# Opening order of a fused attention and two-MLP kernel: w_out converted one block later, low parts on VectorE, x parts and weight sums made beside the last plain slices, loads held during bursts

## The chip, the core and the metric

The kernel runs on one core of one Trainium2 chip. The metric is the device time of one execution in microseconds, lower is better; it is given as the median of several runs. The engines are named TensorE (matmul; the profile's PE), VectorE (DVE), ScalarE (ACT), GpSimd (POOL) and SyncE (SP, which only issues transfers). TensorE's clock is granted by the chip at one of two levels, 1.2 or 2.4 GHz.

## What is computed

Chunked attention over q, k, v (8 batches, 8 heads, 576 positions, 64 features, chunks of 64), then two gated products one after the other on 4608 tokens of 512 features:

```python
x   = attention(q, k, v)                      # (4608, 512)
x2  = ((x @ w_a) * (x @ w_b)) @ w_out         # 512 -> 1536 -> 512
h   = ((x2 @ w1) * (x2 @ w2)) @ w3            # 512 -> 1024 -> 1024
out = h @ w_out2                              # 1024 -> 512
```

All is float32. The kernel fuses w3 and w_out2 into one matrix first.

## The kernel before, in words

**Numbers.** A float32 product is made of three products of rounded halves: every operand is split into a high part (a ScalarE copy that rounds) and a low part (source minus high part, on VectorE or GpSimd). `split` does both. The raw weights reach the core in another number format and are converted (`Conv`: `s1` is two VectorE operations and a ScalarE one, `s2` a third VectorE operation, L209 to L220). `Pump` runs these conversions as a list of jobs in order: `load` asks for the raw tile, `begin` does `s1`, `run` finishes the job before, does `s2` and hands the result to the job's sink. A w_a or w_b tile is split and its float32 form stored to `d32`; a w_out tile (`out_job`, L745) is split and stored to `dwo`.

**Tokens.** 4608 tokens are 9 blocks of 512. Blocks 0 and 1 are done plainly, one feature block f of 128 at a time (`plain_step`): two banks, `pa` and `pb`, get x @ w_a and x @ w_b, ScalarE copies `pa` to `sa`, VectorE multiplies `pb` by it. For T=0 (block 0) the product is split (`g_parts`) and goes through w_out at once as a `Second`, four parts of three matmuls one step later ("pending"). For T=1 (block 1) it is kept in a `G` tile. The 24 slices run in the order of `plain_order`: five of T=0 first (`AHEAD`), then mixed; the last four are (0, 11), (1, 9), (1, 10), (1, 11). The other blocks go in pairs through Strassen's scheme, seven products where eight would be needed (`strassen_step`), whose x parts come from `strassen_pieces`: 8 differences ("formed") and 14 splits ("one") per pair of blocks, 22 pieces. The sums of weights that the scheme needs are made by `Sums` in the first such block (four adds, two splits and two stores for each f) and reloaded from `dw` later (`load_part`).

**Bursts.** Block j + 1 of a pair has its G tiles multiplied by w_out in one go, `burst` (12 Second products for the first matrix, 8 for the second), before the next pair starts. During a burst VectorE makes the x parts of the next pair, GpSimd the low parts of the G tiles (`ready`), and SP loads `wo` tiles (`Outs.ahead`): four buffers, the last four w_out tiles are still there at the first burst, so its fifth product is the first that needs a load.

**Attention.** A `Unit` is one pair of heads of one token block: load1 (q and k), load2 (v), turn (transposes), scores, soft1, soft2, flip, apply, put. Units 0 to 3 are block 0, units 4 to 7 block 1 (class `First`); the units of the next pair run beside the slices and steps, from fourth product on also in a burst. Loads of q, k and v are put into a list (`ask`), and `tick` issues a few of them with each product; `settle` issues all up to the one needed. While `state["hold"]` is set, `tick` issues none; `burst` sets it at its start and clears it after its first product. `next_units` appends the requests of the next pair's first two units; for the second pair these are 52, put in at slice (1, 9) and issued nine per product (`pace`).

**Order.** Nothing is scheduled by a compiler: each engine runs its instructions in the order in which the program emits them. `Track` spreads pieces of other work over the points of a step: each piece has a cost, and at each `point()` pieces are emitted until their share is done. SP, VectorE and the others each are one queue, in which a waiting instruction holds up all behind it. A tile's buffer is its `tag`: a new tile with the same tag waits for the last reader of the old one.

Of the kernel before, what the change touches and what calls it, by code (L numbers as in the profile page):

```python
# [17 lines left out]
P = 128  # L18
# [92 lines left out]
def chunk_attention_two_gated_products(  # L111
# [434 lines left out]
    class First(TurnedOnPE):  # L546
# [3 lines left out]
        def queues(self):  # L550
            early = self.T == 0 and self.hp < 2
            return nc.sync, *[nc.scalar if early else nc.sync] * 2
# [52 lines left out]
    def strassen_pieces(x32, nm, single=False, diffs=None):  # L605
# [8 lines left out]
        def minus(a, b, name):  # L614
            t = diffs.popleft() if diffs else tmp(name, W)
            nc.vector.tensor_tensor(t, a, b, op=ALU.subtract)
            return t
# [23 lines left out]
        def one(p, kt):  # L641
# [5 lines left out]
        order = [  # L647
            (formed, "P5"),
            (formed, "P6"),
            (one, "P5"),  # L650
            (one, "P1"),
            (one, "P2"),
            (formed, "P7"),
            (one, "P6"),
            (formed, "P4"),
            (one, "P3"),
            (one, "P7"),
            (one, "P4"),
        ]
        return parts, [  # L660
            (0.7, False, lambda do=do, p=p, kt=kt: do(p, kt)) for do, p in order for kt in range(2)
        ]

# [81 lines left out]
    def out_job(f):  # L745
        def sink(w):
            t = pool.tile([P, 2, DM], F32R, tag=f"wo{f % 4}", name=f"wo_{f}")
            wouts[f] = t

            def low():  # L750
                nc.gpsimd.tensor_tensor(t[:, 1], w, t[:, 0], op=ALU.subtract)
                store(dwo[0][f], t.bitcast(F32), 2, nc.gpsimd)

            return (lambda: nc.scalar.copy(t[:, 0], w)), low

        return (row_conv(w_o, f, f"o{f}"), sink)
# [52 lines left out]
    class Sums:  # L809
# [66 lines left out]

        def early_pieces(self):
            return [
                (1.7, False, self.add),
                (0.7, False, lambda: self.own(0)),  # L880
                (0.4, False, lambda: self.own(1)),
                (0.7, False, lambda: self.early(0)),
                (0.7, False, lambda: self.early(1)),
            ]
# [40 lines left out]
    class Second:  # L925
# [6 lines left out]
        def part(self):  # L932
            m, ph, f, w, g = self.m, self.ph, self.f, self.w, self.g
            if m == 4:
                return
# [105 lines left out]
    def plain_step(ph, j, T, f, nm, point, gplaces, sums, tags, xq=None, freed=None):  # L1041
# [5 lines left out]
        pa = bank(tags[0], f"pa{nm}")  # L1047
        first(w, 0, xq, f"pa{nm}", pa)
# [5 lines left out]
        pb = bank(tags[1], f"pb{nm}")  # L1054
        first(w, 1, xq, f"pb{nm}", pb)
# [8 lines left out]
        else:  # L1064
            nc.vector.tensor_tensor(sa, pb, sa, op=ALU.mult)
            engines.computed(0.7)
            g = g_parts(sa, nm, nc.gpsimd)
# [5 lines left out]
            wo = state["outs"].next() if "outs" in state else wouts[f]  # L1073
# [10 lines left out]
    def burst(ph, j, order, gplaces, others, at, first=None):  # L1084
# [10 lines left out]
        for f in range(n):  # L1095
# [10 lines left out]
            if f == 0:  # L1106
                state["pending"].rest()
                parts.append(ready(ph, j, order[2], gplaces))
                state["hold"] = False
# [91 lines left out]
    with tc.manual_schedule():  # L1201
# [4 lines left out]
        for f in range(NF[0]):  # L1206
            pump.add(pair_jobs(f) + [out_job(f)])
# [58 lines left out]
        asked(U[0].load1, U[1].load1)  # L1266
        pump.load()
        asked(U[2].load1, U[3].load1, U[2].load2)
# [16 lines left out]
        AHEAD = 5  # L1285
# [6 lines left out]
        asked(U[0].load2)  # L1292
# [5 lines left out]
        asked(U[1].load2)  # L1298
        U[1].scores()
        U[2].turn()  # L1300
        U[0].soft2()
        U[0].flip()
        U[1].soft1()
        pump.load()
        asked(U[4].load1)
        U[1].soft2()
# [3 lines left out]
        U[3].turn()  # L1310
        U[1].flip()
        U[2].soft1()
        pump.run()
# [22 lines left out]
        def features(m, kks):  # L1336
            terms = [(wp, xp, kk) for kk in kks for wp, xp in SEQ[::-1]]
            some(pairs[0, 0], m, xq, banks[m], terms, kks[0] == 0, kks[-1] == KM - 1)

# [8 lines left out]
        pump.ahead = 2  # L1348
# [8 lines left out]
        pump.ahead = 1  # L1357
        pump.run()
        U[4].soft1()
        pump.flush()  # L1360
        nc.vector.tensor_tensor(sa, banks[1], sa, op=ALU.mult)  # L1361
        state["pending"] = Second(0, 0, 0, wouts[0], g_parts(sa, "0_0_0", nc.gpsimd), sums[0])
        pump.ahead = 2
# [8 lines left out]
        at = None  # L1372
        for n, (T, f) in list(enumerate(order))[1:]:
            if T == 0:
                ahead = f + 1 < AHEAD
                conv = Track([conv_piece()] * (4 if f == 1 else 3), 2 if ahead else 8, engines)
                if f + 1 == NF[0]:
                    conv = None
            if T == 1 and f == 0:
                late.finish()  # L1380
                at = Track(both[cut:], sum(3 if T_ else 5 for T_, _ in order[n:-3]) - 2, engines, 3.0)

            def point(pe=True):
                if conv:
                    conv.point(pe)
                (at or late).point(pe)

            if T == 1:
                for i in [f + 1] if f else [0, 1]:
                    for m in range(2 if i < NF[0] else 0):  # L1390
                        store(dw[0][i][m], whole(pairs[0, i][m]).bitcast(F32), 2, nc.gpsimd)
            if n + 3 == len(order):
                at.finish()
                next_units(2)
                state["pace"] = 9
            if n + 1 == len(order):
                state["ready"] = ready(0, 1, NF[0] - 2, plain[0])
            plain_step(0, 0, T, f, f"0_{T}_{f}", point, plain[0], sums[0], "AC")
# [3 lines left out]
        at.finish()  # L1402

# [15 lines left out]
        def block_steps(ph, sb, x, at):  # L1419
# [10 lines left out]
            for k, f in enumerate(order):  # L1430
                extra = None
                if new:
                    if k + 2 < n:
                        su[k + 2] = summed(ph, order[k + 2], k + 2)
                        su[k + 2].load()
                    extra = Track(su[k + 1].pieces() if k + 1 < n else [], 5, engines, 2.0)
# [7 lines left out]
                def freed(i):  # L1444
                    if k + 2 < n:
                        if whole_new and f + 2 >= READY:
                            return
                        if not new or i in (0, 3):
# [10 lines left out]
                if k + 1 == n and ph == 0 and sb + 1 < NSB:  # L1459
                    for a in at:  # L1460
                        a.finish()
                    next_units(sb + 2)
# [67 lines left out]
        for ph, sb in [(0, sb) for sb in range(1, NSB + 1)] + [(1, sb) for sb in range(NSB + 1)]:  # L1530
# [13 lines left out]
            elif not begins:  # L1544
                x, pieces = strassen_pieces(x32, f"{ph}{sb}", sb == NSB)
            if ph == 0 and sb == 1:
                for n_ in range(2):
                    first_sums[n_] = summed(ph, orders[ph, sb][n_], n_)
                    first_sums[n_].load()
                    for i in (0, 3):  # L1550
                        load_part(ph, orders[ph, sb][n_], i)
                pieces = pieces + first_sums[0].pieces()
# [54 lines left out]
            j, places = block_steps(ph, sb, x, at)  # L1607
# [51 lines left out]
```

## Time and profile before

| | us |
|---|---|
| median of 3 runs | 1606.45 (1604.29 to 1608.12) |
| profiled execution | 1609.44 |
| its span, first to last instruction | 1607.6 |
| mean granted TensorE clock in it | 0.985 of 2.4 GHz |

The profile is of one execution. A line of the timeline gives an instruction, or several alike merged (x8), with start and duration, and in brackets how long its engine was idle before it and what ended that. `SPq`, `ACTq` and the like are an engine's queue issuing a transfer. TensorE's busy time is the sum of its matmuls, which are pipelined, so a busy TensorE at half clock counts as busy too.

### The profile page before, as it was taken

To read this page: it belongs to the slowest core of one execution; us is meant where nothing else is said; L and a number is where in the kernel's file an instruction comes from. 1 tells how busy PE (TensorE), PEld (TensorE's weight loads), DVE (VectorE), ACT (ScalarE), POOL (GpSimd) and SP (SyncE) were. 2 spreads that over 40 slices of the span, in tenths; PEclk is the share of its full clock that TensorE was granted. 3 is DMA by queue.
4 is the path that set the end of the run, shared out by engine and by line. 5 is a ranking of instruction groups with operands and counts; after the bars stand their busy time and mean duration, and the time that the engine had idled before them with its cause. 6 is when DMAs were issued, how large, how long until landed. Compare 5 with 4: busy or idle time off the path is not lost.

```text
span 1607.6 us, 24155 instructions
## 1 busy us (share of the span) xinstructions
PE 1545.6 (96%) x8968; PEld 1255.6 (78%) x8968; DVE 859.0 (53%) x1384; ACT 538.4 (33%) x997; POOL 492.6 (31%) x502
## 2 busy tenths in 40 slices
PE   5799999899899999999999999999999999999998
PEld 4578787677677788887877888888878878878887
DVE  4877564677757555476776345634632432432431
ACT  3544344322233222342334323333421321421322
POOL 0323224222234111343224312224522422422422
PEclk8899999899999999999999999999999999999999
DMA  8798756677646787569985899777366266166184
GB/s 229 230 263 267 245 154 226 211 226 222 208 151 188 203 222 231 142 200 337 323 315 184 296 335 356 288 262 261 112 230 216 76 227 219 68 222 205 68 294 152
DMA packets 277014, 356.31 MB, mean 222 GB/s; under 512 B 174241, under 2 KB 194721, under 8 KB 276897
## 3 DMA queue, kind: packets, MB, share of 16 engines
q1 hardware_dynamic: 244448, 261.43, 52.7%
q0 software_dynamic: 23616, 81.80, 13.3%
q10 hardware_dynamic: 8832, 11.54, 2.1%
q8 instruction: 71, 1.16, 0.3%
q14 instruction: 47, 0.38, 0.1%
HBM read 268.70 MB, written 85.98 MB: 221 GB/s over the span
## 4 chain that ended last, share of the span: by engine, by line
PE 81%; DVE 7%; DMA 4%; issue 3%; ACT 2%; SPq 1%; POOL 1%; DVEq 0%; ACTq 0%; POOLq 0%
PE P L914 39%; PE acc L944 23%; PE pa L901 4%; PE pb L901 4%; PE wf L1189 3%; PE pb0L L901 2%; PE pa0L L901 2%; DVE xP L288 2%; DMA wo<-dwo 2%; PE x L442 1%; SPq L181 1%; PE s L390 1%; DMA qk<-in_k_dram 1%; DMA v<-in_v_dram 1%; ACT xP L287 1%
## 5 line engine op out<-in xcount | busy, mean ns | idle before, releaser
L914 PE MATMUL P<-xP,w 128*128 128x512 f32 (+1 forms) x3066 | 695.3, 380 | 13.5 <-DVE c L1034 5.2
L914 PEld LDWEIGHTS P<-xP,w 128*128 128x128 f32 x3066 | 550.7, 188 | 130.3 <-DVE c L1034 7.5
L1005 DVE TENSOR_TENSOR c<-P,c 128x512 f32<-128x512 f32 (+1 forms) x228 | 150.0, 661 | 320.4 <-PE P L914 319.7
L1001 ACT COPY c<-P 128x512 f32<-128x512 f32 (+1 forms) x228 | 128.2, 563 | 212.7 <-PE P L914 211.5
L1036 POOL TENSOR_TENSOR G<-c,c 128x512 f32<-128x512 f32 x68 | 90.7, 1334 | 312.3 <-DVE c L1005 312.2
L287 ACT CAST gh<-c 128x512 fp32r<-128x512 f32 x68 | 42.2, 621 | 325.2 <-DVE c L1034 325.1
L288 POOL TENSOR_TENSOR gl<-c,gh 128x512 fp32r<-128x512 f32 x68 | 90.7, 1333 | 191.5 <-ACT gh L287 186.0
L944 PE MATMUL acc<-gh,wo 128*128 128x512 f32 x384 | 138.2, 400 | 0.0
L1034 DVE TENSOR_TENSOR c<-P,c 128x512 f32<-128x512 f32 x68 | 47.0, 691 | 124.7 <-PE P L914 124.6
L944 PE MATMUL acc<-wo,gh 128*128 128x512 f32 x320 | 111.0, 390 | 0.5 <-ACT gh L287 0.5
L944 PEld LDWEIGHTS acc<-gh,wo 128*128 128x128 f32 x384 | 72.6, 189 | 15.7
L901 PE MATMUL pa<-xq,w 128*128 128x512 f32 x276 | 72.4, 414 | 6.3 <-DVE w L725 6.3
L288 DVE TENSOR_TENSOR xP<-xP,xP 128x512 fp32r<-128x512 f32 (+1 forms) x56 | 65.7, 1217 | 21.2 <-ACT xP L287 21.2
L944 PE MATMUL acc<-gl,wo 128*128 128x512 f32 x192 | 75.4, 393 | 0.0
L944 PEld LDWEIGHTS acc<-wo,gh 128*128 128x128 f32 x320 | 60.1, 188 | 12.9 <-ACT gh L287 1.0
L901 PE MATMUL pb<-xq,w 128*128 128x512 f32 x276 | 68.8, 398 | 0.8 <-DVE sa L1361 0.8
L901 PEld LDWEIGHTS pa<-xq,w 128*128 128x128 f32 x276 | 53.1, 197 | 19.0 <-DVE w L725 6.9
L954 ACT COPY ev<-acc 128x512 f32<-128x512 f32 x72 | 42.3, 587 | 72.5 <-PE acc L944 67.6
L944 PE MATMUL acc<-wo,gl 128*128 128x512 f32 x160 | 62.5, 390 | 0.8 <-POOL gl L288 0.8
L901 PEld LDWEIGHTS pb<-xq,w 128*128 128x128 f32 x276 | 50.9, 190 | 11.9 <-DVE sa L1361 1.3
L190 POOL DMA_DIRECT2D dw<-w x58 | 31.8, 551 | 91.0 <-DVE w L288 83.0
L408 ACT ACTIVATE e<-e 128x512 f32<-128x512 f32 x36 | 22.8, 634 | 102.2 <-DVE e L402 98.4
(163 smaller groups left out, 2368.0 us busy)
## 6 DMA issues: line engine op xcount, KB each, us to landing
w<-dw SPq DMA_DIRECT2D x175, 512.0 KB, 4.6
wo<-dwo SPq DMA_DIRECT2D x128, 512.0 KB, 4.3
dw<-w POOLq DMA_DIRECT2D x58, 512.0 KB, 4.8
w<-dw SPq DMA_DIRECT2D x59, 256.0 KB, 3.6
su<-d SPq DMA_DIRECT2D x20, 512.0 KB, 5.4
x2d<-ev POOLq DMA_DIRECT2D x36, 256.0 KB, 4.3
x<-x2d SPq DMA_DIRECT2D x36, 256.0 KB, 4.4
out_dram<-ev POOLq DMA_DIRECT2D x36, 256.0 KB, 2.9
```

Source lines behind the costliest of these rows:

```text
L190: queue.dma_start(to, src)
L287: nc.scalar.copy(dst_h, src)
L288: eng_l.tensor_tensor(dst_l, src, dst_h, op=ALU.subtract)
L901: nc.tensor.matmul(ps, w[m][:, kk // 2, wp, kk % 2], xq[kk // 2][:, kk % 2, xp], start=(begins and n == 0), stop=(ends and n == len(terms) ...
L914: nc.tensor.matmul(ps, w[:, wp, kt], x[:, kt, xp], start=(begins and n == 0), stop=(n == 5), skip_group_check=True,)
L944: nc.tensor.matmul(acc[m], a, b, start=(f == 0 and (wp, gp) == SEQ[0]), stop=(f == NF[ph] - 1 and (wp, gp) == SEQ[-1]),)
L954: nc.scalar.copy(t, acc[m])
L1001: nc.scalar.copy(t, src)
L1005: nc.vector.tensor_tensor(o, a, b, op=ALU.add)
L1034: nc.vector.tensor_tensor(g, last, c11, op=ALU.mult)
L1036: nc.gpsimd.tensor_tensor(g_place(ph, nm.split("_")[0], f, gplaces), c22, c12, op=ALU.mult)
L1189: nc.tensor.matmul(ps, t[:, gp, jj], wo2[jj // 2][:, jj % 2, wp], start=(jj == 0 and (wp, gp) == SEQ[0]), stop=(jj == NF[1] - 1 and (wp, g ...
```

## The change

- `First.queues`: unit 0's values are loaded on GpSimd's queue and unit 1's on SP's instead of both on ScalarE's, and both are asked for near the start.
- The jobs of the pump: w_out tile f is converted after w_a and w_b of f + 1. `Second` takes its w_out tile when it starts (`lambda: wouts[f]`).
- Low parts of w_out 0 to 3 and of the hidden tiles of the first slices (f below 5) are made by VectorE instead of GpSimd. The first conversions are begun one ahead instead of two; slices 4 and 10 get four conversions, the others three.
- The first products of slice (1, 0) are issued three matmuls at a time between the last pieces of attention of block 1.
- For EARLY = 3 feature blocks (11, 10, 9) the weight sums are made beside the last four slices into `xo4` to `xo6` and stored to `dw`; the first pair of Strassen blocks reloads them (`load_part` for i = 0 to 3). Two of the three sums' loads share buffer Y0.
- 18 of the 22 x pieces of the first pair are made beside the last three slices, with differences in `Y2`. Before every later pair but the last of each matrix, 8 of 22 pieces are made in the last step ahead of the burst.
- `hold` is cleared after product n - 4 of a burst instead of the first (n = 12 or 8).

```diff
         def queues(self):
-            early = self.T == 0 and self.hp < 2
-            return nc.sync, *[nc.scalar if early else nc.sync] * 2
+            first = self.T == 0
+            return (
+                nc.sync,
+                nc.scalar if first and self.hp < 2 else nc.sync,
+                nc.gpsimd if first and self.hp == 0 else nc.sync,
+            )
...
+    def diff_tiles(name):
+        t = pool.tile([P, 4, NT], F32, tag="Y2", name=name)
+        return deque([*(t[:, i] for i in range(4)), *[None] * 4])
...
             def low():
-                nc.gpsimd.tensor_tensor(t[:, 1], w, t[:, 0], op=ALU.subtract)
+                e = nc.vector if f + 1 < AHEAD else nc.gpsimd
+                e.tensor_tensor(t[:, 1], w, t[:, 0], op=ALU.subtract)
...
+        def staged_pieces(self, tag):
+            def stage():
+                t = pool.tile([P, 2, 4 * NT // 2], F32R, tag=tag, name=f"st{self.f}")
+                self.stage = [
+                    t[:, i].rearrange("p (o s k n) -> p o s k n", o=2, s=2, k=2) for i in range(2)
+                ]
+            return [
+                (1.7, None, lambda: (stage(), self.add())),
+                (0.7, None, lambda: self.parted(0, self.stage[0])),
+                (0.7, None, lambda: self.parted(1, self.stage[1])),
+            ]
...
+        if begun:
+            pa, pb = begun.banks
+            tick(loads=2)
+            begun(0, [KM - 1])
+        else:
+            pa = bank(tags[0], f"pa{nm}")
+            first(w, 0, xq, f"pa{nm}", pa)
...
-            g = g_parts(sa, nm, nc.gpsimd)
+            g = g_parts(sa, nm, nc.vector if early else nc.gpsimd)
...
                 parts.append(ready(ph, j, order[2], gplaces))
+            if f == n - 4:
                 state["hold"] = False
...
-            pump.add(pair_jobs(f) + [out_job(f)])
+            pump.add(pair_jobs(f) + ([out_job(f - 1)] if f else []))
+        pump.add([out_job(NF[0] - 1)])
...
-        asked(U[0].load1, U[1].load1)
+        asked(U[0].load1, U[0].load2, U[1].load1)
         pump.load()
-        asked(U[2].load1, U[3].load1, U[2].load2)
+        asked(U[2].load1, U[1].load2, U[3].load1, U[2].load2)
...
-                conv = Track([conv_piece()] * (4 if f == 1 else 3), 2 if ahead else 8, engines)
+                pump.ahead = 1 if ahead else 2
+                conv = Track([conv_piece()] * (4 if f + 1 in (AHEAD, NF[0] - 1) else 3), 2 if f < AHEAD else 8, engines)
...
             if T == 1 and f == 0:
-                late.finish()
+                xq = [quadrants[1, 0], quadrants[1, 1]]
+                banks = [bank("AC"[m], f"p{m}1") for m in range(2)]
+                chunks = deque((m, [kk]) for kk in range(KM - 1) for m in range(2))
+                while late.left:
+                    piece = late.left.popleft()
+                    piece[2]()
+                    if piece[1] and chunks:
+                        features(*chunks.popleft())
...
+            if n + 4 == len(order):
+                staged = []
+                for i in range(EARLY):
+                    su = Sums(0, NF[0] - 1 - i, dict(tag=f"Y{i % 2}"))
+                    staged.append((0.1, None, su.load))
+                    staged.append(su.staged_pieces(f"xo{4 + i}"))
+                loads = [staged[2 * i] for i in range(EARLY)]
+                pieces = loads[:2]
+                for i in range(EARLY):
+                    pieces += staged[2 * i + 1] + loads[i + 2 : i + 3]
+                st = Track(pieces, 8, engines)
             if n + 3 == len(order):
                 at.finish()
                 next_units(2)
                 state["pace"] = 9
+                got_x, got_pieces = strassen_pieces(
+                    [u.x32 for u in units], "01", diffs=diff_tiles("xd01"),
+                    steps="f5 f6 o1 o2 o3 f7 o7 f4 o4 o5 o6",
+                )
+                state["parts"] = got_x, got_pieces[18:]
+                xt = Track(got_pieces[:18], 8, engines)
...
-                if k + 1 == n and ph == 0 and sb + 1 < NSB:
+                if k + 1 == n and sb + 1 < NSB:
                     for a in at:
                         a.finish()
-                    next_units(sb + 2)
+                    if ph == 0:
+                        next_units(sb + 2)
+                    steps = "f5 f6 o5 o1 o2 f7 o6 f4 o3 o7 o4"
+                    nx, np = strassen_pieces(
+                        next_x32(), f"{ph}{sb + 1}", diffs=diff_tiles(f"xd{ph}{sb}"), steps=steps
+                    )
+                    state["parts"] = nx, np[8:]
+                    extra = Track(np[:8], 6, engines)
...
             if ph == 0 and sb == 1:
                 for n_ in range(2):
-                    first_sums[n_] = summed(ph, orders[ph, sb][n_], n_)
-                    first_sums[n_].load()
-                    for i in (0, 3):
+                    for i in range(4):
                         load_part(ph, orders[ph, sb][n_], i)
-                pieces = pieces + first_sums[0].pieces()
```

## Rows read from the trace of the kernel before

**Rows 1.** The page's first part: busy us of each engine, share, instructions.
```profile
PE 1545.6 (96%) x8968; PEld 1255.6 (78%) x8968; DVE 859.0 (53%) x1384; ACT 538.4 (33%) x997; POOL 492.6 (31%) x502
```
**Rows 2.** Stretches: length, busy PE PEld DVE ACT POOL; last clock, DMA share, GB/s.
```profile
0.00:120.00 120.00, 89.61 (x850) 70.81 (x851) 83.80 (x160) 54.72 (x108) 26.98 (x37) 0.87 0.84 241
40.00:100.00 60.00, 50.23 (x361) 39.09 (x358) 52.40 (x88) 32.51 (x64) 21.29 (x23) 0.91 0.80 242
280.00:300.00 20.00, 14.13 (x81) 10.73 (x81) 17.49 (x32) 4.57 (x8) 6.44 (x6) 0.79 0.57 170
380.00:420.00 40.00, 35.09 (x235) 26.90 (x233) 27.80 (x52) 8.57 (x17) 9.55 (x10) 1.00 0.72 217
500.00:520.00 20.00, 16.87 (x92) 12.95 (x91) 11.21 (x19) 3.93 (x7) 5.21 (x6) 0.83 0.55 147
```
**Rows 3.** Waits of PE, 0 to 120 us: us in total, times, longest.
```profile
PE pa L901 <- DVE w L725: 6.3, 2, 3.9
...
PE x L442 <- DMA v<-in_v_dram: 3.1, 2, 1.7
```
**Rows 4.** Timeline of ScalarE, 10 to 17 us: start, duration, instruction.
```profile
15.86 0.97 ACTq L181 DMA_DIRECT2D v<-in_v_dram  x2
```
**Rows 5.** Timeline of VectorE, 22 to 29 us.
```profile
28.14 0.76 DVE L400 TENSOR_REDUCE mx<-s 128x4 f32<-128x256 f32 x2 [4.66 <-PE s L390]
```
**Rows 6.** Timeline of GpSimd and of VectorE, 70 to 76 us.
```profile
72.19 1.45 POOL L288 TENSOR_TENSOR gl<-sa,gh 128x512 fp32r<-128x512 f32 x1 [4.36 <-ACT gh L287]
...
71.81 0.70 DVE L212 SCALAR_TENSOR_TENSOR cv_xo<-cv_xo 128x512 int32<-128x512 int32 x1
72.42 1.77 DVE L220 SCALAR_TENSOR_TENSOR cv_Y<-cv_Y,cv_Y 128x512 int32<-128x512 int32 x1
```
**Rows 7.** Timeline of TensorE, 102 to 115 us.
```profile
106.52 0.63 PE L530 MATMUL f<-ident,e 128*128 128x128 f32 x4 [1.86 <-DVE e L416]
...
108.88 5.54 PE L901 MATMUL pa<-xq,w 128*128 128x512 f32 x12
```
**Rows 8.** The chain that ended last: start, us, what.
```profile
205.18 2.72 PE acc L944 x12
...
258.95 5.76 PE acc L944 x24
```
**Rows 9.** Timeline of VectorE, 239 to 260 us.
```profile
247.33 0.69 DVE L1061 TENSOR_TENSOR G0p<-pb,sa 128x512 f32<-128x512 f32 x1 [7.97 <-PE pb L901]
```
**Rows 10.** Groups of VectorE, 258 to 292 us: busy us, mean ns, idle before.
```profile
L288 DVE TENSOR_TENSOR xP<-xP,xP 128x512 fp32r<-128x512 f32 x8 | 9.2, 1197 | 4.5 <-ACT xP L287 4.5
```
**Rows 11.** Timeline of VectorE, 286 to 291 us.
```profile
286.30 0.41 DVE L827 TENSOR_TENSOR su<-su 128x256 f32<-128x256 f32 x1
...
289.28 0.70 DVE L378 STREAM_TRANSPOSE qT<-qk 128x512 f32<-128x512 f32 x1
```
**Rows 12.** Timeline of SP, 221 to 263 and 286 to 300 us.
```profile
220.96 4.05 SPq L181 DMA_DIRECT2D qk<-in_q_dram  x8
...
249.59 6.45 SPq L181 DMA_DIRECT2D v<-in_v_dram  x10
...
262.04 0.32 SPq L782 DMA_DIRECT2D wo<-dwo  x1
...
290.60 0.86 SPq L181 DMA_DIRECT2D qk<-in_q_dram  x2
```
**Rows 13.** Transfers, 255 to 300 us: rate in 40 slices; sums' loads, us to landing.
```profile
GB/s 43 65 266 357 339 219 379 404 408 408 412 415 138 7 58 342 66 211 255 117 346 33 335 102 138 328 0 0 0 0 0 259 339 303 297 296 254 291 118 42
...
su<-d SPq DMA_DIRECT2D x2, 512.0 KB, 5.0
```
**Rows 14.** Timeline of VectorE, 460 to 520 us.
```profile
504.09 0.70 DVE L378 STREAM_TRANSPOSE qT<-qk 128x512 f32<-128x512 f32 x1
```
**Rows 15.** Timeline of SP, 477 to 506 us.
```profile
478.57 4.12 SPq L181 DMA_DIRECT2D qk<-in_q_dram  x7
```
**Rows 16.** Waits of PE, 1150 to 1200 us.
```profile
PE P L914 <- DVE c L1005: 0.8, 1, 0.8
```

## What is predicted, and why

> **What bounds the kernel now.** I read the page's busy line first [rows 1]: TensorE works 1545.6 us of a 1607.6 us span. The change takes no matrix product away, so all that it can win is the 62 us in which TensorE stands still and the time in which its clock is granted at 1.2 instead of 2.4 GHz. The second view is the busy time by stretch [rows 2]: the reader sees where those 62 us lie. The opening (0 to 120) has 30.4 of them, 280 to 300 another 5.9, 380 to 420 some 4.9, 500 to 520 3.1. In all of these but 380 to 420 the mean granted clock is below 1.00 too, as TensorE has just stood idle. Third, the waits name what ends the idle time in the opening: the values `v` and converted weights [rows 3].
>
> The loss around a burst is idle time plus the share of the clock that was not granted. At the end of the first burst that is 5.87 + 0.21 x 20 = 10.1 us, at the end of the second 3.13 + 0.17 x 20 = 6.5 us [rows 2].
>
> **The change part by part, 1: the opening.** Three edits meet here.
>
> (a) The values of units 0 and 1. ScalarE's queue issues them behind its own copies now, those of unit 1 at 15.86 us, which holds the next copy back by 0.97 us [rows 4]. TensorE waits 3.1 us for `v` [rows 3], and VectorE stands idle 4.66 us, until 28.14, since the scores behind that wait come late [rows 5]. Afterwards unit 0's values are issued at the start on GpSimd's queue, unit 1's on SP's ahead of unit 3's q and k: behind about 2.3 MB at 241 GB/s [rows 2], so there by some 13 us (an estimate). I take 4 off, ends 0 and 4.7. The Trainium skill, "DMA: Bandwidth & Descriptors", section "Issuing engines are not separate DMA queues", speaks against a gain from another queue: all issuers share the same 16 DMA engines, so only issue time is saved. By it alone this edit would bring ScalarE's issue time, 2 x 0.97 = 1.9 us; I stay at 4 because the order of the loads changes too.
>
> (b) The low parts of `w_out` 0 to 3 and of five hidden tiles go from GpSimd to VectorE, 9 instructions. VectorE pays 0.70 us each, as for its other operations of that size [rows 6]: 6.3. But a GpSimd subtraction lengthens what VectorE does beside it: the L220 that starts 0.23 us after one takes 1.77 us [rows 6], 1.07 more than its neighbour. I found such a stretched operation beside nearly all of the ten subtractions up to 108 us. So 9 x (0.70 - 1.0) = -2.7; ends +6.3 if the relief fails, -3.3 if each gives 1.07. I take -2.
>
> (c) `w_out` 0 is converted behind `w_a` and `w_b` 1. TensorE waits 6.3 us for a converted `w` [rows 3]. But VectorE is busy 52.4 of 60 us here [rows 2], so a new order mostly moves the queue: by the first slice of T=1 both kernels have converted 17 tiles. I take -1, ends 0 and -4.
>
> Sum of part 1: -7, from +3 to -12.
>
> **2: the first slice of T=1.** Unit 7's chain of transposes, softmax and values is emitted whole before it now; TensorE stands 1.86 us in front of one link and then does twelve matmuls in 5.54 us [rows 7], twice the 2.72 us of others [rows 8]. After, six groups of three matmuls stand between the links. If the clock then stays at 2.4 GHz, the slice ends 5.54 - 2.72 = 2.8 earlier for the clock and up to 1.9 for the wait. But slice 4 has four conversions pressed into its first two points, which can hold unit 7 up: -3.5, from 0 to -4.7.
>
> **3: the last slices and the first burst, the term that decides.** Into the slices go, for each of three feature blocks, a load of 512 KB, four adds, two splits and two stores, and 18 of 22 x pieces; these leave the burst. VectorE has gaps of 7.97 us before the first of those slices' multiplications [rows 9] and of some 2 x 2.72 - 0.69 = 4.75 between them. Work there should cost 0.7 per piece, not the 1.2 that it takes in the burst beside GpSimd [rows 10]. The load is 3 x (4 x 0.41 + 2 x 0.7) + 18 x 0.7 = 21.7 us [rows 6, 11] in four slices that hold about 22. It fits, tightly: the multiplication that frees TensorE's second bank queues behind the pieces, so I put 2 us of TensorE waits on the slices. Without those pieces unit 0's transposes, now at 289.28 [rows 11], come early; SP's q load and with it the `wo` load behind it waits for them until 290.60 [rows 12], and hold keeps such loads off SP anyway. So the 10.1 us at the burst's end go; if that were all, the burst would win 8.
>
> But SP is in order, and the sums' loads stand ahead of 52 requests for q, k and v. SP issues those 52 from 220.96 to 256.04 now, then weights, and at 262.04 the `wo` of the burst's fifth product [rows 12], which is needed at 258.95 + 5 x 2.72 = 272.6 (four products and the pending one before it) [rows 8]. After, SP meets first the load of block 11's sums, which waits until that block's float32 store has landed: about 232 (an estimate: that conversion ends at some 227, and a load of this size lands in 5.0 us [rows 13]). Then comes the load of block 9, whose buffer is block 11's: free only after that block's second split, which is emitted behind the first product part of slice (0, 11), at about 238, and follows the 5.0 us load, four adds and a split: about 241.5. Only then come the 52 requests, 20 us later than now. At the 0.51 us of the first eight they need 27 us, at today's mean 35 [rows 12]: done at 268 to 277. Behind them stand eight weight loads of 3.67 MB, 9.0 us at the 408 GB/s of that stretch [rows 13], then the `wo`: landed at 278 to 290. With the slices 2 us late, TensorE stands from 274.6 for 4 to 15 us. I take 9, and 4 for the low clock behind it, as the 5.87 us of idle time cost today. The term: -10.1 + 2 + 9 + 4 = +5, ends -9 (no such wait) and +11.
>
> **4: the second burst.** Eight of 22 x pieces move into the step ahead; 8 x 1.2 = 9.6 us less lie ahead of unit 0's transposes at 504.09 [rows 14], and no q load that waits for them stands ahead of a `wo` load. Of 6.5 lost I take 5, ends -6.5 and 0 (the 16 q and k loads of unit 1 now come ahead of the last `wo`).
>
> **5: the three bursts of the second product.** Each is followed by one wait of 0.8 us for VectorE [rows 16]. Less work there, eight pieces more in the step ahead: -1.5, ends -2.4 and +1.5.
>
> **6: held requests in the third burst and in blocks** (0, 1) to (0, 3). SP gets 25 requests out in the step before a burst; the others start eight products later. The 4.9 us at 380 to 420 [rows 2] lie in the middle of a block, where nothing changes, and stay. 0, from -3 to +4.
>
> Sum: -7 - 3.5 + 5 - 5 - 1.5 + 0 = -12. The profiled execution took 1609.44 us for its 1607.6 span, 3.0 above the median of the three runs; the difference goes onto the median: 1606.45 - 12 = **1594**.
>
> **The rivals.** First, SP's backlog is gone before the fifth `wo`: part 3 gives -9, and the whole 1606.45 - 7 - 3.5 - 9 - 5 - 1.5 = 1580. For it: eight requests take only 4.05 us when nothing disturbs them [rows 12], and weights could land faster. Against: block 9's buffer, which the code ties to block 11's. Second, VectorE's sum of work binds the opening and the relief fails: part 1 is +2 instead of -7, about 1603, no change. For it: 52.4 of 60 us [rows 2]. Against: the stretched operation [rows 6]. Third, slower: the held requests. Unit 1's transposes sit in VectorE's one queue ahead of the adds of the next block's first step. Today its q loads go out from 478.57 in the second burst [rows 15]; held, they start at about 498 (the eighth product), take 16 x 0.5 us and land near 509, while the shortened burst ends at about 511. From some 4 us later on TensorE waits for each us; at 8 us in each of the first two blocks and 4 in the third, in place of what parts 4 and 6 give, the time is 1594 + 5 + 20 - 5 = 1614. Against it: the air of 4 us, and that the first burst's units are asked for long before it.
>
> **How the numbers follow.** The forecast 0.55 (1586 to 1602), the first rival 0.22 (1574 to 1586), the second 0.13 (1600 to 1608), the third 0.10 (1608 to 1618). A measurement of this kernel tells about 0.2%, 3.2 us, from no change. The range 1577 to 1606 leaves out the best third of the first rival, the top of the second and the third. Faster 0.80 (forecast, first rival, some of the second), same 0.11, slower 0.09.
>
> **What would show it.** Right: VectorE's gap at 23 to 28 us is gone; L220 is near 0.7 in the opening; the first T=1 slice has no matmuls at half speed; SP's 52 requests begin about 20 us later against slice (0, 11); one wait for `wo` at the fifth product of the first burst; unit 0's transposes in the second burst come some 9 us earlier. Wrong: no such `wo` wait (then 1580), TensorE idle in slices 9 to 11 by over 4 us, or VectorE waiting for k in the first step of a block (then near 1614).

## The result, and the profile after

| | before | after |
|---|---|---|
| median, us | 1606.25 (1604.29 to 1608.12) | 1623.32 (1619.28 to 1629.74) |
| profiled execution, us | 1609.44 | 1622.68 |
| its span, us | 1607.6 | 1620.9 |
| granted clock | 0.985 | 0.983 |

The changed kernel is slower: ratio 1.0117, 95% interval 1.0096 to 1.0139. 1594 was predicted, with a range up to 1606. The page's busy line, the same five stretches as in [rows 2], and TensorE's waits:

```profile
PE 1544.8 (95%) x8968; PEld 1255.7 (77%) x8968; DVE 855.7 (53%) x1393; ACT 538.9 (33%) x997; POOL 478.4 (30%) x495
```
```profile
0.00:120.00 120.00, 87.54 (x843) 68.36 (x844) 77.37 (x162) 53.77 (x104) 13.27 (x28) 0.89 0.82 229
40.00:100.00 60.00, 46.85 (x340) 35.21 (x338) 45.52 (x88) 29.35 (x55) 6.47 (x12) 0.91 0.72 218
280.00:300.00 20.00, 3.02 (x11) 2.17 (x10) 3.15 (x4) 0.67 (x2) 2.65 (x2) 0.61 0.73 272
380.00:420.00 40.00, 39.64 (x286) 31.36 (x285) 31.27 (x57) 12.39 (x24) 11.30 (x12) 1.00 0.84 248
500.00:520.00 20.00, 20.00 (x118) 16.36 (x117) 11.88 (x17) 6.14 (x11) 8.26 (x6) 1.00 0.55 173
```

TensorE's work is what it was [rows 1]; the 13.3 us of span are idle time. In 40 to 100 TensorE and VectorE both did less than before (46.85 and 45.52 us against 50.23 and 52.40), so the sum of work of neither set the time there; e1 below shows that a chain between engines did. From 280 to 300 TensorE worked 3.02 us, at 0.61 of its clock.

The milestones say in which stretch the time changed (us; TensorE's first instruction of each where nothing else is said; "joined" is the run e5 below):

| | before | after | after - before | joined |
|---|---|---|---|---|
| first features | 35.15 | 31.37 | -3.8 | 31.60 |
| slice (0, 5) | 117.71 | 119.41 | +1.7 | 111.56 |
| first burst | 258.95 | 265.70 | +6.8 | 258.66 |
| block (0, 1) | 304.98 | 324.14 | +19.2 | 296.80 |
| last product of block (0, 1) starts | 472.7 | 485.4 | +12.7 | 457.9 |
| block (0, 2) | 517.2 | 530.2 | +13.0 | 496.7 |
| end of the span | 1607.6 | 1620.9 | +13.3 | 1586.2 |

So the first burst lost 12.4 us, the opening lost 1.7 where 10.5 were to be won, the slices lost 5.1 more (6.8 - 1.7), and block (0, 1) gave 6.5 back (19.2 to 12.7). From slice (0, 5) to the burst TensorE waits 1.6 us for a probability copy and 0.8 and 3.0 us for VectorE's products, where before it waited 0.9 us once.

**The opening.** TensorE's waits up to 120 us, then what VectorE's conversions (L220) waited for from 38 to 108 us, by form with busy time, mean ns and idle time before:

```profile
PE acc L960 <- DVE wo L752: 9.1, 4, 3.9
PE x L442 <- ACT pT L533: 8.0, 4, 5.1
```
```profile
L220 DVE SCALAR_TENSOR_TENSOR cv_xo<-cv_xo,cv_xo 128x512 int32<-128x512 int32 x8 | 5.5, 689 | 3.8 <-ACT cv_xo L215 3.8
L220 DVE SCALAR_TENSOR_TENSOR cv_Y<-cv_Y,cv_Y 128x512 int32<-128x512 int32 x7 | 4.8, 690 | 5.2 <-ACT cv_Y L215 5.2
```

A conversion goes from VectorE (L212) to ScalarE (L215) and back to VectorE (L220). VectorE stood still for 9.0 us (3.8 + 5.2) at that return. Before the change, in the same stretch, it stood there for 0.8 us, while the operations themselves took longer (1172 and 997 ns against 689 and 690):

```profile
L220 DVE SCALAR_TENSOR_TENSOR cv_xo<-cv_xo,cv_xo 128x512 int32<-128x512 int32 x8 | 9.4, 1172 | 0.8 <-ACT cv_xo L215 0.8
L220 DVE SCALAR_TENSOR_TENSOR cv_Y<-cv_Y,cv_Y 128x512 int32<-128x512 int32 x7 | 7.0, 997 | 0.0
```

The timeline of VectorE after the change shows one instance:

```profile
49.74 0.69 DVE L212 SCALAR_TENSOR_TENSOR cv_xo<-cv_xo 128x512 int32<-128x512 int32 x1
51.16 0.69 DVE L220 SCALAR_TENSOR_TENSOR cv_xo<-cv_xo,cv_xo 128x512 int32<-128x512 int32 x1 [0.72 <-ACT cv_xo L215]
51.77 0.68 DVE L752 TENSOR_TENSOR wo<-cv_xo,wo 128x512 fp32r<-128x512 f32 x1
```

With one conversion begun ahead there is nothing between L212 and L220 of the same tile. The w_out tile behind it comes 0.72 us later here, and TensorE waits for such tiles four times, 9.1 us in all.

**The first burst.** The timeline of SP, and of TensorE at the burst's fifth product:

```profile
229.13 5.11 SPq L820 DMA_DIRECT2D su<-d  x2
234.28 2.60 SPq L181 DMA_DIRECT2D v<-in_v_dram  x3
245.74 0.33 SPq L820 DMA_DIRECT2D su<-d  x1
246.12 6.59 SPq L181 DMA_DIRECT2D qk<-in_q_dram  x8
...
277.55 6.76 SPq L181 DMA_DIRECT2D v<-in_v_dram  x10
284.42 1.49 SPq L798 DMA_DIRECT2D w<-dw  x3
...
289.42 2.10 SPq L783 DMA_DIRECT2D wo<-dwo  x3
```
```profile
298.52 0.77 PE L960 MATMUL acc<-gh_1b,wo 128*128 128x512 f32 x1 [16.98 <-DMA wo<-dwo]
```

SP stands in front of each of the three sums' loads: for the landing of a store (8.4 us), for a conversion that still uses the buffer (4.3) and for VectorE's work on the first sums (9.0, until 245.74). Its waits from 220 to 250 us:

```profile
SPq L820 <- DVE su L828: 9.0, 1, 9.0
SPq L820 <- DMA d<-cv_Y: 8.4, 1, 8.4
SPq L820 <- DVE cv_Y L220: 4.3, 1, 4.3
```

The 52 requests behind the third load are out at 284.3, the `wo` load goes at 289.42 instead of 262.04 [rows 12], and TensorE waits 16.98 us.

### The profile page after: what moved, and what is told of

It reads as the page before. It is cut to its first block, busy times and chain, and to the rows that moved or that the text cites. A ratio compares the mean times of both kernels' runs of the same rounds, so it can differ in the third digit from the quotient of the medians.

```text
span 1620.9 us, 24171 instructions
## 1 busy us (share of the span) xinstructions
PE 1544.8 (95%) x8968; PEld 1255.7 (77%) x8968; DVE 855.7 (53%) x1393; ACT 538.9 (33%) x997; POOL 478.4 (30%) x495
## 4 chain that ended last, share of the span: by engine, by line
PE 85%; DVE 5%; DMA 4%; SPq 3%; issue 2%; ACT 2%; POOL 0%; POOLq 0%; DVEq 0%; ACTq 0%
PE P L928 40%; PE acc L960 27%; PE pa L915 3%; PE pb L915 3%; PE wf L1214 3%; SPq L181 2%; PE pb0L L915 2%; PE pa0L L915 2%; PE x L442 1%; PE s L390 1%; DMA wo<-dwo 1%; PE t L519 1%; PE p L915 1%; DMA v<-in_v_dram 1%; DMA su<-d 1%
## 5 line engine op out<-in xcount | busy, mean ns | idle before, releaser
L960 PEld LDWEIGHTS acc<-gh,wo 128*128 128x128 f32 x384 | 73.8, 192 | 26.9 <-DVE wo L752 6.5
L288 DVE TENSOR_TENSOR xP<-xd,xP 128x512 fp32r<-128x512 f32 x32 | 55.7, 1778 | 47.9 <-ACT xP L287 47.8
L915 PE MATMUL pa<-xq,w 128*128 128x512 f32 x264 | 65.3, 396 | 1.9 <-ACT w L729 1.9
L915 PEld LDWEIGHTS pa<-xq,w 128*128 128x128 f32 x264 | 48.6, 188 | 12.6 <-ACT w L729 2.0
L960 PE MATMUL acc<-gh_1b,wo 128*128 128x512 f32 x96 | 33.6, 427 | 19.9 <-DMA wo<-dwo 17.0
```

The lines of the kernel that those rows point to most:

```text
L288: eng_l.tensor_tensor(dst_l, src, dst_h, op=ALU.subtract)
L915: nc.tensor.matmul(ps, w[m][:, kk // 2, wp, kk % 2], xq[kk // 2][:, kk % 2, xp], start=(begins and n == 0), stop=(ends and n == len(terms) ...
L960: nc.tensor.matmul(acc[m], a, b, start=(f == 0 and (wp, gp) == SEQ[0]), stop=(f == NF[ph] - 1 and (wp, gp) == SEQ[-1]),)
```

## The experiments

"Joined" stands for the changed kernel with the edits of e1, e3 and e4 together. Ratios are to the kernel before, with 95% intervals.

**e1: conversions begun two ahead.**

```diff
-                pump.ahead = 1 if ahead else 2
+                pump.ahead = 2
```

> The changed kernel with the conversions of slices 1 to 4 begun two ahead again, as before, instead of one. Theory A (begin-ahead): with one ahead VectorE waits 9.0 us in 38 to 108 for ScalarE's step inside the conversion it has just begun (L215), and the late w_out tiles and w tiles follow from that; expected: these waits fall to under 2 us, TensorE's 9.1 us of waits for w_out shrink to under 4, slice (0, 5) starts 6 to 9 us earlier than at 119.4, and the time is 1614 to 1617 against 1623 of the changed kernel. Theory B (job order): w_out one job later is what makes TensorE wait; expected: waits for w_out stay at 7 or more, slice (0, 5) within 2 us of 119.4, time 1621 to 1624.

1617.89 us, ratio 1.0076 (1.0052 to 1.0100), span 1617.1. VectorE's groups from 38 to 108 us:

```profile
L220 DVE SCALAR_TENSOR_TENSOR cv_xo<-cv_xo,cv_xo 128x512 int32<-128x512 int32 x8 | 5.5, 685 | 0.0
L220 DVE SCALAR_TENSOR_TENSOR cv_Y<-cv_Y,cv_Y 128x512 int32<-128x512 int32 x7 | 4.8, 686 | 1.6 <-ACT cv_Y L215 1.6
```

The stall at the return fell from 9.0 to 1.6 us and TensorE's waits for w_out from 9.1 to 2.0 us, slice (0, 5) starts at 111.76 instead of 119.41, and block (0, 1) 10 us earlier. By the end of the span 3.8 us of it are left; most of the difference goes in block (0, 2), where TensorE waits 2.2 us for VectorE once, between 543 and 563 us, and the granted clock is 0.93 from 563 to 583 (after has neither).

**e2: the old order of conversions, one begun ahead.**

```diff
-            pump.add(pair_jobs(f) + ([out_job(f - 1)] if f else []))
+            pump.add(pair_jobs(f) + [out_job(f)])
...
```

With the order come back a third conversion run ahead of the slices and the old number of conversions in slices 1, 4 and 10.

> The changed kernel with the order of the conversions as before (w_a, w_b, w_out of the same block, a third run in the opening, four conversions in slice 1 and none pressed into slice 4), everything else as changed, conversions still begun one ahead. Theory A (begin-ahead): the waits of VectorE for ScalarE stay near 9 us; TensorE's waits for w_out go, waits for w come back in their place, slice (0, 5) starts within 3 us of 119.4, time 1620 to 1625. Theory B (job order): waits for w_out (9.1) and the 5.1 us wait for the transposed p in slice 4 go, slice (0, 5) starts 6 to 12 us earlier, time 1611 to 1617.

1627.57 us, ratio 1.0135 (1.0104 to 1.0166), slice (0, 5) at 122.59, 3.2 later than after. The waits for w_out are gone and waits for the converted w of 8.4 us stand in their place. So the order is not the cause of the loss. The times of the two kernels are too close to tell apart, but slice (0, 5) says that the order helps, and e10 says the same.

**e3: the three staged loads of sums on GpSimd's queue.**

```diff
-                    staged.append((0.1, None, su.load))
+                    staged.append((0.1, None, lambda su=su: su.load(nc.gpsimd)))
```

> The changed kernel with the three early loads of the weight sums issued on GpSimd's queue instead of SP's. Theory C (SP's order): the third load holds SP until 245.7, the 52 requests end at 284.4 and the burst's fifth w_out load is issued at 289.4, so TensorE waits 17.0 us; with the three loads off SP the requests start near 221, the w_out load is issued before 275, the wait is under 3 us, and the first burst ends 17 to 21 us earlier; of that 3 to 7 may be lost again in the next block, whose gain of 6.6 us came from SP being ahead; time 1604 to 1610. Rival D (bytes): the 3.67 MB of weight loads and the many small requests are too much wherever the sums' loads stand; the wait stays above 8 us and the time above 1614.

1605.69 us, ratio 1.0007 (0.9989 to 1.0025). SP's timeline, and TensorE's waits from 262 to 310 us:

```profile
223.88 4.05 SPq L181 DMA_DIRECT2D qk<-in_q_dram  x8
...
257.48 9.14 SPq L181 DMA_DIRECT2D v<-in_v_dram  x10
...
271.94 11.52 SPq L783 DMA_DIRECT2D wo<-dwo  x3
```
```profile
PE acc L960 <- DMA wo<-dwo: 1.0, 1, 1.0
```

The requests go out 22 us earlier, the wait is 1.0 instead of 17.0, and block (0, 1) starts at 306.83 instead of 324.14. The bytes are the same: what cost the time was the order on one issuing queue. The 22 us are SP's three waits of 21.7 us (8.4 + 4.3 + 9.0), which have gone with the loads. The Trainium skill, "DMA: Bandwidth & Descriptors", section "Issuing engines are not separate DMA queues", says that issuing from several engines saves only the time to initiate a transfer, usually small against the transfer itself. This run gained something else. The 52 requests stayed on SP and took it 42.7 us (223.88 to 266.62) instead of 38.2 (246.12 to 284.31), and the three loads cost SP 0.3 us each to issue; what the move took off SP was the waiting in front of them.

**e4: hold ended after the first product, as before the change.**

```diff
-            if f == n - 4:
-                state["hold"] = False
+                state["hold"] = False
```

(The line goes back under `if f == 0`.)

> The changed kernel with the hold of the requests cleared after a burst's first product, as before. Theory E (held requests): the second burst's wait of 4.46 us for a w_out load comes from 17 requests that unit 1's transposes force onto SP ahead of it; with early release they are out before; expected: that wait under 1.5 us, time 3 to 5 us lower, 1618 to 1620; the first burst's 17 us stay, since its requests are all issued before it. Rival: the release lets q loads wait on SP for unit 0's transposes again, as before (1.4 us); no change of time, 1621 to 1625.

1618.33 us, ratio 1.0089 (1.0056 to 1.0122). From the start of the last product of block (0, 1) to block (0, 2) it takes 39.2 us instead of 44.9 (44.5 before the change), with no wait of TensorE in it. After the change there was one, behind requests that the hold had kept back (TensorE's waits, and SP's timeline):

```profile
PE acc L960 <- DMA wo<-dwo: 4.5, 1, 4.5
```
```profile
514.12 4.05 SPq L181 DMA_DIRECT2D qk<-in_q_dram  x8
518.21 3.90 SPq L181 DMA_DIRECT2D qk<-in_k_dram  x8
522.21 0.38 SPq L783 DMA_DIRECT2D wo<-dwo  x1
```

The first burst's wait, 18.1 us, is unchanged: another cause.

**e5: the three together (joined).**

> The changed kernel with the three cures together: conversions begun two ahead in the slices, the staged loads of the sums requested from GpSimd's queue, and the hold ended after the first product of a burst. Theory: the three losses lie in three places (38 to 108 us, the first burst, the second burst), so what they gave singly adds: spans 3.8, 13.3 and 5.3 us shorter, from 1620.9 to about 1598.5, some 1600 us of time (1596 to 1602), below both kernels. Rival 1: an earlier slice stage only brings TensorE sooner to the same load, so the 3.8 is lost again: about 1604. Rival 2: the 6 us that e1 gave back after the first burst were given back only through the late out weights, so the whole 10 us come: about 1593.

1590.89 us, ratio 0.9911 (0.9879 to 0.9944), span 1586.2: faster than both kernels, and the second rival's time. The single runs' medians lie 5.4, 17.6 and 5.0 us under the changed kernel's, 28.0 together; the joined one 32.4. The first burst takes 38.1 us; before it took 46.0.

**e6: joined, with the nine low parts on GpSimd again.**

> The kernel of e5_join with the nine early low-part subtractions (four of w_out's tiles, four or five of the products' G) on GpSimd again, as before the change; everything else stays. Theory (the subtraction on GpSimd slows VectorE's operations beside it): VectorE's subtractions of line 220 in the slices go from about 0.69 to 1.0 to 1.2 us again, and the kernel is 2 to 4 us slower than e5_join. Rival (the work is only handed from an idle engine to one that is wanted): no difference, or up to 3 us faster than e5_join.

1589.31 us, ratio 0.9901 (0.9869 to 0.9932). VectorE's groups, 38 to 108 us:

```profile
L220 DVE SCALAR_TENSOR_TENSOR cv_xo<-cv_xo,cv_xo 128x512 int32<-128x512 int32 x8 | 11.0, 1369 | 0.0
L220 DVE SCALAR_TENSOR_TENSOR cv_Y<-cv_Y,cv_Y 128x512 int32<-128x512 int32 x7 | 8.1, 1157 | 1.5 <-ACT cv_Y L215 1.5
```

The operations do stretch beside GpSimd, by 8.8 us in all (19.1 against 10.3). As VectorE has nine subtractions less to do, it is busy for 80.7 us up to 112 us instead of 76.7 in e5. Yet slice (0, 5) starts at 111.31, as with the edit (111.56): VectorE had room for the 4.0 us.

**e7: joined, with the fifth slice's conversions spread over three points.**

> The kernel of e5_join with the four conversion steps of the fifth slice spread over three places instead of two. Theory: the 5.1 us in which TensorE waits for the copy of a transposed probability tile comes from the conversions pressed ahead of that copy on ScalarE's queue; with the last of them behind another point the wait shrinks by one to two conversions (1.2 to 2.5 us), and the kernel is 1 to 2.5 us faster than e5_join. Rival: the copy waits for something else, the wait stays at 5 us and the time within 0.5 us.

1591.78 us, ratio 0.9917 (0.9886 to 0.9948); TensorE's wait for the probability copy stays at 5.1 us. A miss, and no test of its theory: in the traces of e5 and e7 TensorE, VectorE, ScalarE and GpSimd compute the same instructions in the same order. The edit moved one request for v on SP and no conversion, so e7 is close to a second e5. It shows how far two profiles of nearly the same program lie apart: 8.5 us in span (1594.7 against 1586.2). In this run's profile block (0, 1) takes 7.4 us more than in e5 (168.5 against 161.1) although nothing in it was edited: TensorE waits 3.1 us for VectorE until 427.06, and the granted clock from 420 to 440 is 0.83.

**e8: joined, without the eight x pieces ahead of the later bursts.**

```diff
-                    state["parts"] = nx, np[8:]
-                    extra = Track(np[:8], 6, engines)
+                    state["parts"] = nx, np
```

> The kernel of e5_join with the first eight joined x pieces back in the burst, as before the change, instead of in the last step of the block ahead. Theory (the pieces ahead of a burst relieve VectorE in it): each of the later bursts is 1 to 3 us longer by waits of TensorE for VectorE's products, some 3 to 6 us in all. Rival (a burst is bound by TensorE's own products and the pieces are hidden either way): within 1 us of e5_join.

1604.73 us, ratio 1.0002 (0.9983 to 1.0021): 13.8 us slower than e5, over twice the upper end of what I expected. The spans differ by 13.3 us: 11.4 of them lie in four bursts, and 1.7 come before slice (0, 5), where the two kernels are the same. From the last product of block (0, 1) to (0, 2) there are 43.4 us instead of 38.8, with the waits of before the change back: 1.7 us for unit 0's transposes and 2.4 us for a `wo` load. The third burst takes the same time in both. Three bursts of the second product cost 29.1 us each instead of 26.8, with waits that e5 does not have (TensorE's waits, 1130 to 1165 us):

```profile
PE acc L960 <- POOL gl_1b L288: 1.9, 1, 1.9
```

This is not the kernel of before in those bursts: there they took 27.4 us with no piece made ahead. e8 keeps the differences in `Y2`; whether that is what makes it slower than before was not tested.

**e9: joined, with the opening's loads and steps as before the change.**

> The kernel of e5_join with the opening's loads and their steps as before the change: v of the first two heads' units requested later and from ScalarE's queue, the probability tiles turned and the first conversion run in the old order. Theory (the earlier v brings the first features 3.8 us forward, and TensorE keeps what it is given once conversions are begun two ahead): 3 to 4.5 us slower than e5_join, and slice (0,5) starts 3 to 4 us later than 111.6. Rival (a later wait, the 5.1 us for a turned probability tile near 91 us or the start of the first burst, takes it back): the fifth slice and the time within 1.5 us of e5_join.

1597.08 us, ratio 0.9956 (0.9936 to 0.9976). The medians lie 6 us apart, but the profile shows little: first features at 32.39 against 31.60, slice (0, 5) at 112.22 against 111.56, span 1589.0 against 1586.2; the profiled execution is the fastest of its runs, in both. VectorE's largest gap from 18 to 28 us is 1.97 us, not the 4.66 of [rows 5], without the new place of v; with it, in e5, it is 3.09.

**e10: joined, with the old order of conversions** (and their old numbers per slice, as in e2).

> The kernel of e5_join with w_out's tiles converted in their old place, ahead of the next slice's pair, so that only the order of conversions is undone and they are still begun two ahead. Theory (the order alone brings each pair of w1 and w2 tiles forward, worth about 1 us a slice at most): 1 to 4 us slower, TensorE's waits for the converted pair above 4 us. Rival (with two begun ahead the order matters no longer): within 1 us of e5_join.

1597.42 us, ratio 0.9951 (0.9928 to 0.9974). Slice (0, 5) starts at 116.14, 4.6 later than in e5. TensorE's waits from 38 to 118 us:

```profile
PE pa L915 <- ACT w L729: 4.9, 1, 4.9
...
PE pa L915 <- DVE w L725: 1.7, 1, 1.7
```

**e11: joined, without the staged weight sums.**

> The kernel of e5_join without the weight sums made beside the last plain slices: the first three blocks' sums are loaded, added and split in the first burst and in the block, as before the change. Theory (the work leaves a burst and a block that VectorE bounds): the first burst is 3 to 6 us longer than e5_join's, block (0,1) gets back waits for VectorE's products of 3 to 6 us, the slices win 2 to 3 us back: 4 to 9 us slower in all. Rival (the sums were hidden where they stood and the gain of the changed first burst comes from the joined x pieces alone): within 2 us.

1587.18 us, ratio 0.9903 (0.9884 to 0.9923). The first burst starts at 254.24 instead of 258.66 and takes 37.6 instead of 38.1 us; block (0, 1), first to last product, takes 165.9 instead of 161.1. What the staging took from the slices, 4.4 us, the block gave back: 4.7. The burst had room for the sums all along. From slice (0, 5) to the burst the slices take 142.0 us here with the 18 x pieces still in them, 141.2 before the change and 147.1 in e5: of the added work the sums cost TensorE time there, the x pieces hardly any.

**e12: what is left of the change.** Conversions two ahead, old hold, low parts on GpSimd, no staged sums; kept are the loads of the opening, the order of conversions, the features issued in groups, and the x pieces.

> What the other runs leave of the change: conversions begun two ahead, the hold ended after the first product of a burst, low parts on GpSimd as before, the weight sums made in the first burst and in block (0,1) as before; kept are the opening's loads, the later conversion of w_out's tiles, the first product of the sixth slice run in pieces, and the joined x pieces ahead of the bursts. Theory (low parts and staged sums carry nothing; order, x pieces and hold carry the gain): 1585 to 1591, 0.9 to 1.3% under the kernel before, no slower than e5_join. Rival (the two edits each hide a part of the other's cost, so that without both a wait comes back): 1593 or more.

1589.54 us, ratio 0.9903 (0.9876 to 0.9929). No slower than the joined kernel: the low parts on VectorE and the staged sums can go too.

## Why the prediction was wrong, point by point

The sum was -12; the profiles stand 13.3 us apart on the other side. Of the 25 us between, parts 1 and 2 are 12.2, part 3 is 12.5 and part 4 is 5.4; block (0, 1) gave 6.5 back that no part had promised, which is luck as far as the forecast goes.

**Parts 1 and 2, predicted -7 and -3.5; they came to +1.7.** The failed step is one that was not priced: the opening begins one conversion ahead instead of two. Part 1 named three edits and took this fourth at nothing. It costs 7.7 us with the new order (119.41 against 111.76) and 6.5 with the old (122.59 in e2 against 116.14 in e10). Its trace was readable beforehand: L220's idle time of 0.8 us was small because other work lay between L212 and L220. With two ahead the opening does win: 117.71 to 111.56, -6.2 of the -10.5. The second rival's +2 for part 1 lies near the measured +1.7 by chance, for its cause is another. Split by what each single undoing gives back at slice (0, 5) (in e1, e5, e7, e8 and e11, which hardly differ up to there, it starts between 111.56 and 113.25, so a difference under 1.7 us says nothing):

| term | predicted | measured |
|---|---|---|
| (a) v earlier | -4 | -0.7 (e9) |
| (b) low parts on VectorE | -2 | +0.3 (e6) |
| (c) w_out later | -1 | -4.6 (e10) |
| first slice of T=1, with whatever else is left | -3.5 | -1.2 |

In (a) I gave a gap on VectorE the value of a gap on TensorE; the first features came 3.8 earlier, but e9 has most of that without the new loads. The gap itself shrank from 4.66 to 3.06 us and did not go. In (b) the relief was real and of the predicted size (8.8 us for nine subtractions), yet bought nothing: the rival "VectorE's sum of work binds the opening" had its premise wrong, too. In (c) "a new order mostly moves the queue" was wrong: 6.6 us of waits for w in e10 stand against 2.2 in e5, which has 2.3 for w_out instead, and the measured 4.6 lies near the end of 4. By their own terms the ends of part 1 add up to +6.3, not +3. In part 2, of the six groups of matmuls two stand between links at half speed (1.63 and 1.44 us for three each) and the other four run together (18 matmuls with the rest in 4.38 us): 7.5 us where there were 8.4.

**Part 3, predicted +5; it came to +17.5 (12.4 in the burst and 5.1 in the slices).** The mechanism is the one told, and the mis-sized term is the wait for `wo`: the third sums' load stops SP, the 52 requests follow (246.12 for the predicted 241.5), and the fifth product waits for `wo`. The size was wrong: 17.0 us where 9 was taken, past the end of 15. The tile came at 298.5, 14.5 later than the middle of the estimate (284): the requests started 4.6 later than the 241.5 taken, the 52 took 38 us where 27 to 35 stood in the bounds, and from the last of them to the tile it took 14.2 where 10 to 13 were left. TensorE needed the tile at 281.5, 6.9 later than the 274.6 taken, which hid part of it. Why the requests took longer than in the kernel before (35 us) was not isolated. The slices lost 5.1 us instead of 2, and TensorE stood 5.4 us in the last of them, where over 4 had been named as a sign of being wrong; e11 gives 4.4 of the joined kernel's slices to the staged sums. That the burst without the backlog wins 8 us, the first rival's premise, is borne out: 46.0 to 38.1 in e5.

**Part 4, predicted -5, came to about 0** (517.2 - 472.7 = 44.5 before, 44.9 after). The end named for it, requests ahead of the last `wo`, is what happened (4.5 us). e4 wins 5.6 there, near the predicted size. The part's own mechanism holds: unit 0's transposes come 19.3 us after the block's last product starts instead of 31.4. **Part 5** came as told, -0.5 to -0.6 a burst (26.8 or 26.9 against 27.4).

**Part 6, predicted 0.** The hold cost what stands under part 4, not the waits of TensorE for VectorE that the third rival feared: VectorE did stand 6.1 us for a held q load, until 519.52, but TensorE's wait there was the one for `wo`. That the 4.9 us at 380 to 420 stay was wrong: in the whole of block (0, 1) TensorE waited 8.0 us for VectorE before, and 2.5 after. From its first to its last product block (0, 1) took 167.7 us before, and takes 165.9 and 166.2 in e11 and e12, where the sums are made in it again. The eleven profiles with the sums staged lie from 160.6 to 168.5, median 162.7. So part of the stall seems to belong to the sums, and part comes and goes: e5 and e7 lie 7.4 us apart.

**Why one fix shows little and three show much.** In spans e1 kept 3.8 of 10 us, e3 won 13.3, e4 5.3, 22.4 together, and joined they won 34.7. The surplus of 12.3 us lies mostly in two blocks that no edit touches. Block (0, 2) takes 3.9 us more in e1 than in after, through the wait named there, which the joined profile lacks; block (0, 1) takes 1.5 to 1.8 us more in each of the three single runs than in after, and no more in the joined one. That is 9.7 us with the small differences of block (0, 2), about what the spans of e5 and e7 differ by (8.5), so much of it may be chance. Where the rest is from I did not isolate.

**What stays open:** why e9's median is 6 us above e5's when its profile shows 2.8; and which phase between VectorE and TensorE brings the 2 to 3 us waits inside a block.

## What to carry to other kernels

When work goes from one engine to another and back to the first, count what the first has to do in between; one less tile in flight cost 7.7 us here, more than any reordering of the same work won. Before a load that waits for a buffer is put on a queue, list what stands behind it: moving three loads to another queue won 17 us in the first burst. And an edit that shortens an engine's work is worth something only where that engine is the last that others wait for: 4.0 us less of VectorE's time bought nothing in the opening.

## What the runs showed that I had not expected

- A wait of 2 to 3 us in the middle of a block can cost twice itself: in e7 the 3.1 us in block (0, 1) go with a granted clock of 0.83 over 20 us, 1.2 instead of 2.4 GHz for some of them: 0.17 x 20 = 3.4 us more.
- In the changed kernel SP took 0.5 us for each of eight requests for q in one stretch (4.05 us, at 514.12) and 1.1 us for each of eight for k in another (9.05 us, at 252.75).
- Whether eight x pieces of 22 are made ahead of a burst or in it decides over 11.4 us in four bursts (e8 against e5): 4.6 in the second, 2.2 or 2.3 in each of the three of the second product. The third burst does not change.
